# Seven partial products in place of eight for the second products of two token blocks, in five pairs of layer one

## The chip, the cores and the metric

The kernel runs on one core of one Trainium2 chip. The metric is the device time of one execution, in microseconds (us).

## What is computed

Attention with a cluster mask, then two feed-forward layers on 1536 tokens of 512 features (d_ff 2048):

```python
attn_out = _attn_ref(...)                        # 2 x 8 heads x 768 x 64
x = attn_out.transpose(0, 2, 1, 3).reshape(1536, 512)
h = x @ moe_w_in; g = np.maximum(0.01 * h, h); x = g @ moe_w_out          # layer one
h = x @ moe2_w_in; r = np.maximum(h, 0); out = (r * r) @ moe2_w_out       # layer two
```

## The kernel before

Every product in 32-bit precision is made of three matmuls: each operand is split into a high part (rounded to the matmul's format) and a low part (the rest), and high x high, high x low and low x high are summed in PSUM. A matmul has a stationary operand of 128x128 and a moving one of 128x512.

A layer runs over 16 blocks of 128 hidden features, taken in eight pairs, named by their first block, f = 0, 2, ... 14. The tokens are three blocks of 512 (0, 1, 2). In a pair, the first products make h (features x tokens) from the input x; ScalarE writes the activated high part gh and the activated value itself back to PSUM (`acts`, L912), VectorE subtracts them to the low part gl (L934); the second products (`g2`, L945) multiply g by the output weights into four banks o0 to o3 (512 outputs in four slices of 128), summed over the two blocks of the pair, and `flush` (L999) adds each bank into the accumulator `acc` in SBUF on VectorE (L1005).

The pairs f = 0, 2 and 4 of layer one are plain: 3 token blocks x 2 feature blocks x 4 x 3 = 72 matmuls of first products. From f = 6 on `quad` (L1030) makes the first products of token blocks 0 and 1 as a 2 x 2 product of half matrices by Winograd's form of Strassen's rule: seven partial products P1 to P7 of 6 matmuls instead of eight. They go into the banks U, V, W, X (h0 to h3); ScalarE keeps copies of partial sums (L1045, L1056), VectorE adds them (L1038). It needs sums of the input halves (`t_ops`, L1087, worked off over turns by the table `SUMS`, L1192) and sums of the weights, which are a third weight block beside the pair's two (`sum_pieces`, L207). Token block 2 has 24 matmuls. Second products are 72 in every pair, by the plain rule.

A weight block comes by one DMA of 1 MB (SP's queue) as 64-bit words, which are decoded in pieces (`decode_pieces`, L152): load (piece 0), then ScalarE makes the magnitude into wt (L173) and GpSimd the low word (L180) (piece 1), VectorE joins them (L186, piece 2), ScalarE rounds the high part wh (L147, piece 3), GpSimd subtracts the low part wl (L148, piece 4). A sum block has four sums on GpSimd (L221, piece 0), wh (1) and wl (2). The raw words and the words of each of the two blocks have one buffer each; wh and wl go round a ring of RING buffers.

All engines run their instructions in the written order from pair 2 on (`manual_schedule`). `step_list` (L1151) writes a pair as a list of steps, and the loop at the end puts behind step i the pieces of the next pair's weights (`TURN`, L1181) and the sums that SUMS has for that turn; turns are counted over all steps of a layer (pair 0 has ten, pair 2 twelve). The second products of token block 2 of a pair run in the next pair, between its first products.

Of the kernel before, what the change touches and what calls it, by code (L numbers as in the profile page):

```python
# [8 lines left out]
F32 = mybir.dt.float32  # L9
# [54 lines left out]
)  # L64
DOTS = {(0, 0): 0, (0, 1): 1, (1, 0): 2}


@with_exitstack
def attention_moe_moe_kernel(
# [22 lines left out]
    NBLK = NT // N  # L92
    PLAIN = (3, 1)
    EARLY = 1
    RING = 6
    SIDE = 4

    const = ctx.enter_context(tc.tile_pool(name="const", bufs=1))
    const.tile([128, 88], F32, name="cpad")
    xp = ctx.enter_context(tc.tile_pool(name="xp", bufs=1))  # L100
    rpad = ctx.enter_context(tc.tile_pool(name="rpad", bufs=1, side="right"))
    rpad.tile([128, 120], F32, name="rp")
# [104 lines left out]
    def sum_pieces(ci):  # L207

        st = {}
        K = DM // 2  # L210

        def sums():
            w = st["w"] = stg[1].tile([128, 4, K], F32, tag="ws", name="ws")
            t0, t1 = words.pop(ci - 2), words.pop(ci - 1)
            for o, i, k, op in (
                (w[:, 0], t1[:, 0:K], t1[:, K : 2 * K], ALU.add),
                (w[:, 1], w[:, 0], t0[:, 0:K], ALU.subtract),
                (w[:, 2], t0[:, 0:K], t1[:, 0:K], ALU.subtract),
                (w[:, 3], t0[:, K : 2 * K], w[:, 1], ALU.subtract),
            ):  # L220
# [10 lines left out]
        )  # L231


    ast = ctx.enter_context(ExitStack())
    hbp = ast.enter_context(tc.tile_pool(name="hbp", bufs=1))
# [641 lines left out]
    def bank(i):  # L877
        return ps_h.tile([128, N], F32, tag=f"h{i}", name="h")

    def product(out, w, x, first):  # L880
        n = len(w) * 3
        i = 0
        for (ah, al), (bh, bl) in zip(w, x):
            for l, r in ((ah, bh), (ah, bl), (al, bh)):
                nc.tensor.matmul(  # L885
                    out=out, lhsT=l, rhs=r, start=(first and i == 0), stop=(i == n - 1),
                    skip_group_check=not first,
                )
                i += 1
# [49 lines left out]
    def act(m, b, f, h):  # L939
        for g in acts(m, b, f, h):  # L940
            g()
# [85 lines left out]
            r = b * N + o * 128  # L1027
            nc.sync.dma_start(out=out[r : r + 128, part], in_=ob)

    def quad(m, f):  # L1030
        f0, f1, s = ((m, f, j) for j in range(3))
        k2 = range(2)

        def p(out, w, x, first):
            product(out, [w(k) for k in k2], [x(k) for k in k2], first)

        def add(out, a, b):
            nc.vector.tensor_tensor(out=out, in0=a, in1=b, op=ALU.add)  # L1038
# [112 lines left out]
    def step_list(m, f, prev):  # L1151

        def unit(b, j):
            return lambda: act(m, b, f + j, g1(m, b, f + j))

        def out_of(b, j):
            return lambda: g2(m, b, f + j)

        behind = [lambda q=q: g2(*q) for q in prev]
        tail = [(m, 2, f), (m, 2, f + 1)]  # L1160
        if f < 2 * PLAIN[m]:
            seq = [unit(0, 0), unit(0, 1)]
# [7 lines left out]
        first, second, third = quad(m, f)  # L1170
# [132 lines left out]
```

## Time and profile before

| | us |
|---|---|
| median of 3 runs | 752.75 |
| lowest, highest | 749.59, 754.55 |
| the profiled execution | 749.51 |
| its span | 747.7 |

The span runs from the first to the last instruction; 1.8 us of the profiled execution lie around it. Attention takes the first 243 us or so, layer one some 250, layer two 255. Engines: PE = TensorE matmul, PEld = its weight loads, DVE = VectorE, ACT = ScalarE, POOL = GpSimd, SP = the queue that issues DMAs. L963 is line 963 of the code. An engine's busy time is a mean over stages; where one engine is never idle, the others' idle time costs nothing.

### The profile page before, as it was taken

The page shows a single profiled execution, that of the slowest core. Times are in us where ns is not written, and L with a number is a line of the kernel's source. Part 1 is how long each engine was busy: PE and PEld are TensorE (multiplying, and loading weights), DVE is VectorE, ACT ScalarE, POOL GpSimd, SP SyncE. Part 2 cuts the span into 40 slices and gives each one's busy share as a digit, 9 for nine tenths or more (in the row PEclk, how much of TensorE's full clock was granted, in tenths as well). Part 3 has the DMA queues.
Part 4 walks back from the last instruction along what each step waited for, and adds up shares of the span by engine and source line. Part 5 has one row for each costly group of instructions (what it writes and reads, how often), then busy time and mean ns, then how long its engine had stood idle before and what let it go on. Part 6 is the DMA issues. An engine that isn't in the chain of part 4 may idle for free.

```text
span 747.7 us, 11095 instructions
## 1 busy us (share of the span) xinstructions
PE 740.7 (99%) x4044; PEld 646.1 (86%) x4044; DVE 509.6 (68%) x800; ACT 440.7 (59%) x817; POOL 439.6 (59%) x422
## 2 busy tenths in 40 slices
PE   8999999999999999999999999999999999999998
PEld 8999999999998888888888888888888888888886
DVE  7899999999996335666455454563667666576655
ACT  7988988988997553444344343556644335443430
POOL 9999999999866526654342443499434342343400
PEclk9999999999999999999999999999999999999999
DMA  3684574473503311113111131111212112121004
GB/s 109 172 219 114 117 175 117 112 176 77 148 1 114 112 57 57 56 57 113 57 57 57 57 113 56 57 57 57 73 50 103 57 57 66 50 111 56 1 1 169
DMA packets 16406, 64.78 MB, mean 87 GB/s; under 512 B 3040, under 2 KB 4192, under 8 KB 11360
## 3 DMA queue, kind: packets, MB, share of 16 engines
q1 hardware_dynamic: 16352, 64.07, 28.6%
q8 instruction: 32, 0.52, 0.3%
q14 instruction: 22, 0.18, 0.1%
HBM read 43.02 MB, written 3.15 MB: 62 GB/s over the span
## 4 chain that ended last, share of the span: by engine, by line
PE 92%; ACT 3%; DVE 2%; POOL 1%; issue 1%; DMA 0%; POOLq 0%; ACTq 0%; DVEq 0%
PE o L963 34%; PE h L885 33%; PE A L551 8%; PE S L454 7%; PE T L516 7%; PE S L325 1%; ACT e L486 1%; DVE nm L476 1%; PE o L993 1%; DVE el L533 1%; ACT eh L527 0%; POOL e L503 0%; POOL xl L581 0%; POOL hb L650 0%; POOL xh L229 0%
## 5 line engine op out<-in xcount | busy, mean ns | idle before, releaser
L148 POOL TENSOR_TENSOR wl<-wt,wh 128x1024 fp32r<-128x1024 f32 x32 | 76.9, 2402 | 110.4 <-ACT wh L147 110.4
L934 DVE TENSOR_TENSOR gl<-h,gh 128x512 fp32r<-128x512 f32 x96 | 65.6, 690 | 92.8 <-ACT h L929 74.4
L1005 DVE TENSOR_TENSOR acc<-o,acc 128x512 f32<-128x512 f32 x144 | 94.4, 686 | 27.5 <-PE o L963 27.5
L885 PE MATMUL h<-xh,wl 128*128 128x512 f32 x288 | 112.1, 389 | 0.0
L885 PE MATMUL h<-xl,wh 128*128 128x512 f32 x288 | 112.1, 389 | 0.0
L885 PE MATMUL h<-xh,wh 128*128 128x512 f32 x288 | 111.9, 390 | 0.0
L533 DVE TENSOR_TENSOR el<-T,eh 128x512 fp32r<-128x512 f32 x144 | 94.5, 682 | 2.9 <-ACT eh L527 2.3
L503 POOL TENSOR_SCALAR e<-e,r 128x768 f32<-128x768 f32 x96 | 86.2, 908 | 12.6 <-PE T L516 6.8
L476 DVE TENSOR_REDUCE nm<-S 128x1 f32<-128x768 f32 x96 | 90.8, 947 | 3.5 <-PE S L325 1.8
L486 ACT ACTIVATE e<-S,nm 128x768 f32<-128x768 f32 x96 | 87.2, 908 | 9.8 <-DVE ds L353 5.3
L454 PE MATMUL S<-hb 128*128 128x384 f32 x384 | 89.4, 347 | 0.1
L527 ACT CAST eh<-T 128x512 fp32r<-128x512 f32 x144 | 79.6, 590 | 8.7 <-PE T L516 8.6
L928 ACT ACTIVATE gh<-h 128x512 fp32r<-128x512 f32 x48 | 28.7, 597 | 89.6 <-PE h L885 63.8
L551 PE MATMUL A<-eh,vv 128*128 128x256 f32 x288 | 80.3, 308 | 0.6 <-DVE xt L573 0.6
L516 PE MATMUL T<-ident,e 128*128 128x128 f32 x576 | 79.7, 273 | 0.5 <-POOL e L503 0.5
L963 PE MATMUL o<-gl,wh 128*128 128x512 f32 x192 | 74.7, 389 | 0.0
L963 PE MATMUL o<-gh,wl 128*128 128x512 f32 x192 | 74.7, 389 | 0.0
L963 PE MATMUL o<-gh,wh 128*128 128x512 f32 x192 | 73.7, 389 | 0.0
L551 PE MATMUL A<-el,vv 128*128 128x256 f32 x288 | 73.0, 283 | 0.2 <-DVE el L533 0.2
L516 PEld LDWEIGHTS T<-ident,e 128*128 128x128 f32 x576 | 68.9, 143 | 3.6 <-POOL e L503 0.7
L963 PE MATMUL o<-wh,gh 128*128 128x512 f32 x184 | 71.6, 389 | 0.0
L963 PE MATMUL o<-wl,gh 128*128 128x512 f32 x184 | 71.6, 389 | 0.0
(163 smaller groups left out, 1584.5 us busy)
## 6 DMA issues: line engine op xcount, KB each, us to landing
wraw<-w SPq DMA_DIRECT2D x32, 1024.0 KB, 4.7
hb<-spl SPq DMA_DIRECT2D x14, 576.0 KB, 4.7
hb<-spl SPq DMA_DIRECT2D x42, 192.0 KB, 5.1
rqk<-qk SPq DMA_DIRECT2D x16, 384.0 KB, 3.9
rv<-v SPq DMA_DIRECT2D x8, 384.0 KB, 3.3
out<-q SPq DMA_DIRECT2D x11, 256.0 KB, 2.1
hb<-st SPq DMA_DIRECT2D x56, 24.0 KB, 2.2
out<-q SPq DMA_DIRECT2D x2, 128.0 KB, 1.8
```

What stands on the lines that cost most here:

```text
L148: return lambda: nc.gpsimd.tensor_tensor(out=wl, in0=t, in1=wh.bitcast(F32), op=ALU.subtract)
L454: nc.tensor.matmul(out=s[:, c, 0:HALF], lhsT=hb[:, a, i * 128 : (i + 1) * 128], rhs=hb[:, b, c * HALF : (c + 1) * HALF], start=(a == 0), s ...
L476: nc.vector.tensor_reduce(out=n, in_=s_t[t][:, :, 0:HALF], axis=AX.XY, op=ALU.max, negate=True)
L486: nc.scalar.activation(out=e.rearrange("p (a b) -> p a b", a=2), in_=s_t.pop(t)[:, :, 0:HALF], func=AF.Exp, bias=n_t.pop(t), scale=1.0, ac ...
L503: nc.gpsimd.tensor_scalar(out=e_t[t], in0=e_t[t], scalar1=r_t[t // 2][:, t % 2 : t % 2 + 1], scalar2=1.0, op0=ALU.mult, op1=ALU.mult,)
L516: nc.tensor.transpose(T[:, o : o + 128], e_t[2 * u + b][:, kc * 128 : (kc + 1) * 128], ident)
L527: nc.scalar.copy(out=eh[:, 2 * g : 2 * g + 2, :].rearrange("p a b -> p (a b)"), in_=T_t[u, g])
L533: nc.vector.tensor_tensor(out=el[:, 2 * g : 2 * g + 2, :].rearrange("p a b -> p (a b)"), in0=T_t.pop((u, g)), in1=eh[:, 2 * g : 2 * g + 2, ...
L551: nc.tensor.matmul(out=A, lhsT=w, rhs=m[:, kc, :], start=(kc == 0 and i == 0), stop=(kc == KC - 1 and i == 1),)
L885: nc.tensor.matmul(out=out, lhsT=l, rhs=r, start=(first and i == 0), stop=(i == n - 1), skip_group_check=not first,)
L963: nc.tensor.matmul(out=outs[o], lhsT=l, rhs=r, start=(first and i == 0), stop=(last and i == 2),)
L1005: nc.vector.tensor_tensor(out=a, in0=ps, in1=a, op=ALU.add)
```

## The change

In the pairs f = 4, 6, 8, 10, 12 of layer one (`SEVEN`) the second products of token blocks 0 and 1 are seven partial products M1 to M7 by the same rule: B11, B21 (block 0) and B12, B22 (block 1) are the activated values, T1 to T4 their sums, made on VectorE and split like the others; a fourth weight block (index 3) holds the sums of the output weights. M1, M6, M7, M4 add up in one pair of banks (A: o0, o1), M2, then M5 and M3 in the other (B: o2, o3), and after each the running content is added to `acc` (r1.0 is the flush of M1's first half). Block 2's second products are made in the same pair (o0 to o3 of the list, flushed by f0 to f3), no longer in the next. The whole order of such a pair is one list: n, l, c are pieces of the next pair's, the pair after's and this pair's weight blocks, k copies, a adds, h, f and l behind a name its high part, full value and low part. u0 and u1 (token block 2) share bank h1.

```diff
+SEVEN_REST = (
+    "M1 M2 r1.0 r1.1 r2.0 r2.1 B22l l0.0 u1 u1h u1f u1l n2.0 M6 M5 r6.0 r5.0 r5.1 r6.1 n2.1 n2.2 o0 f0 "
+    "M3 r3.0 T4h T4l r3.1 o1 f1 n3.0 M7 r7.0 r7.1 o2 f2 M4 r4.0 r4.1 o3 f3"
+)
+SEVEN_QUAD = (
+    "n0.1 P1 k1 P2 c3.1 c3.2 n0.2 aV n1.0 P6 k6 B11h B11f P5 k5 B11l n0.3 n0.4 P7 aX B22h B22f P3 aW "
+    "B12f P4 B21h B21f T1 T3 B21l T2 n1.1 T1h T2h T1l n1.2 T4 u0 T2l u0h u0f u0l T3h T3l n1.3 n1.4 "
+) + SEVEN_REST
+SEVEN_PLAIN = (
+    "n0.1 g00 B11h B11f c3.1 c3.2 bh0 n0.2 B11l n1.0 g01 B21h B21f B21l bh1 n0.3 n0.4 g10 B12f T1 n1.1 "
+    "n1.2 g11 B22h B22f T3 T2 T1h T2h T1l T4 u0 T2l u0h u0f u0l T3h T3l n1.3 n1.4 "
+) + SEVEN_REST + " h4.0 h4.1"
...
-    RING = 6
+    RING = 7
+    SEVEN = (4, 6, 8, 10, 12)
...
-    const = ctx.enter_context(tc.tile_pool(name="const", bufs=1))
-    const.tile([128, 88], F32, name="cpad")
+    lpad = ctx.enter_context(tc.tile_pool(name="lpad", bufs=1))
+    lpad.tile([128, 96], F32, name="lp")
...
+    ast = ctx.enter_context(ExitStack())
+    hbp = ast.enter_context(tc.tile_pool(name="hbp", bufs=1))
+    const = ast.enter_context(tc.tile_pool(name="const", bufs=1))
+    const.tile([128, 120], F32, name="cpad")
...
+            if m == 0 and f in SEVEN:
+                blocks.append((m, f, 3))
...
-            t0, t1 = words.pop(ci - 2), words.pop(ci - 1)
+            m, f, j = blocks[ci]
+            t0, t1 = (words[blocks.index((m, f, i))] for i in range(2))
+            if j == 2:
+                a11, a12, a21, a22 = t0[:, 0:K], t0[:, K : 2 * K], t1[:, 0:K], t1[:, K : 2 * K]
+            else:
+                a11, a12, a21, a22 = (
+                    t[:, DM + i * K : DM + (i + 1) * K] for i in range(2) for t in (t0, t1)
+                )
...
-    def quad(m, f):
+    def quad(m, f, behind=True):
...
-            act(m, 0, f, V)
+            if behind:
+                act(m, 0, f, V)
...
                 nc.scalar.copy(out=kept[-1], in_=q)
+            if not behind:
+                act(m, 0, f, V)
...
+    def seven(f, prev, after, later):
...
+        ops["aV"] = lambda: add(get("V"), get("V"), st["k1"])
+        ops["aX"] = lambda: add(get("X"), get("U"), st["k5"])
+        ops["aW"] = lambda: add(get("W"), get("W"), st["k6"])
...
+        def active(n, x, sbuf=False):
+            full[n] = tmp("t", 3) if sbuf else x
+            prelu(full[n], x)
+
+        for n, q in (("B11", "V"), ("B21", "U"), ("B22", "X"), ("B12", "W")):
+            ops[n + "h"] = lambda n=n, q=q: high(n, get(q), True)
+            ops[n + "f"] = lambda n=n, q=q: active(n, get(q), n in ("B11", "B12"))
...
+        ops["T1"] = lambda: t_sum("T1", "B12", "B11", "B11")
+        ops["T3"] = lambda: t_sum("T3", "B22", "B12", "B12")
+        ops["T2"] = lambda: t_sum("T2", "B22", "T1", None)
+        ops["T4"] = lambda: t_sum("T4", "B21", "T2", "B21")
...
+        for n in ("B11", "B21", "B22", "T1", "T2", "T3", "T4", "u0", "u1"):
+            eng = nc.gpsimd if n in ("B11", "T1", "T2", "T3") else nc.vector
+            ops[n + "l"] = lambda n=n, eng=eng: low(n, eng)
...
+        for name, q, block, c, g, b, half in (
+            ("1", "A", f0, DM, "B11", 0, 0), ("2", "B", f1, DM, "B21", 0, 0),
+            ("6", "A", so, K, "T2", 1, 0), ("5", "B", so, 0, "T1", 1, 1),
+            ("3", "B", so, 3 * K, "B22", 1, 0), ("7", "A", so, 2 * K, "T3", 1, 1),
+            ("4", "A", f1, DM + K, "T4", 0, 1),
+        ):
...
-            11: "w12.0 w11.0", 12: "t1.0 w22.0", 13: "t2.0 h1.0", 14: "l1.0 h2.0",
-            15: "t3.0 w21.0", 16: "l2.0 h3.0", 17: "t4.0", 18: "l3.0",
-            22: "w12.1 w11.1", 23: "t1.1 w22.1", 24: "t2.1 h1.1", 25: "l1.1 h2.1",
-            26: "t3.1 w21.1", 27: "l2.1 h3.1", 28: "t4.1", 29: "l3.1", 30: "h4.0", 31: "h4.1",
+            7: "w12.0 w11.0", 8: "t1.0 w22.0", 9: "t2.0 h1.0", 10: "l1.0 h2.0",
+            11: "t3.0 w21.0", 12: "l2.0 h3.0", 13: "t4.0", 14: "l3.0",
+            15: "w12.1 w11.1", 16: "t1.1 w22.1", 17: "t2.1 h1.1", 18: "l1.1 h2.1",
+            19: "t3.1 w21.1", 20: "l2.1 h3.1", 21: "t4.1 l3.1",
...
-            seq, prev = step_list(m, f, prev)
...
+            if m == 0 and f in SEVEN:
+                seven(f, prev, after, later)
+                prev = []
+                continue
+            seq, prev = step_list(m, f, prev)
...
+                if m == 0 and i == 8 and f + 2 == SEVEN[0]:
+                    piece((*after, 3), 0)
```

## Rows read from the trace of the kernel before

**Rows 1.** The page's table of busy time: us, share of the span, instructions.
```profile
PE 740.7 (99%) x4044; PEld 646.1 (86%) x4044; DVE 509.6 (68%) x800; ACT 440.7 (59%) x817; POOL 439.6 (59%) x422
```

**Rows 2.** Busy time by stretch, one pair: busy us (instructions), granted clock, DMA share.
```profile
341.56:372.84 31.28, 31.28 (x140) 25.90 (x139) 16.45 (x24) 13.15 (x20) 12.28 (x10) 1.00 0.20 69
```

**Rows 3.** The chain in order of time, layer one: start, us, what.
```profile
341.56 4.08 PE h L885 x18
...
372.84 4.08 PE h L885 x18
```

**Rows 4.** Timeline, layer one: start us, us, engine, line, operation [idle before].
```profile
333.01 0.39 PE L885 MATMUL h<-xh,wl 128*128 128x512 f32 x1
...
333.50 0.70 DVE L1038 TENSOR_TENSOR h<-h,q 128x512 f32<-128x512 f32 x1 [1.10 <-ACT q L1045]
...
343.89 0.39 PE L885 MATMUL h<-xh,wl 128*128 128x512 f32 x1
344.12 0.39 PE L885 MATMUL h<-xh,wh 128*128 128x512 f32 x1
...
344.32 0.70 DVE L1038 TENSOR_TENSOR h<-h,q 128x512 f32<-128x512 f32 x1 [0.60 <-PE h L885]
...
344.93 0.68 DVE L934 TENSOR_TENSOR gl<-h,gh 128x512 fp32r<-128x512 f32 x1
...
345.05 0.60 ACT L928 ACTIVATE gh<-h 128x512 fp32r<-128x512 f32 x1 [0.22 <-DVE h L1038]
...
345.55 0.59 ACT L929 ACTIVATE h<-h 128x512 f32<-128x512 f32 x1
```

**Rows 5.** Groups of instructions: xcount, busy us, mean ns, idle before; one DMA line.
```profile
L885 PE MATMUL h<-xh,wh 128*128 128x512 f32 x288 | 111.9, 390 | 0.0
...
L1005 DVE TENSOR_TENSOR acc<-o,acc 128x512 f32<-128x512 f32 x144 | 94.4, 686 | 27.5 <-PE o L963 27.5
...
L148 POOL TENSOR_TENSOR wl<-wt,wh 128x1024 fp32r<-128x1024 f32 x32 | 76.9, 2402 | 110.4 <-ACT wh L147 110.4
...
L147 ACT CAST wh<-wt 128x1024 fp32r<-128x1024 f32 x32 | 33.7, 1053 | 1.7 <-DVE wt L186 1.7
...
L221 POOL TENSOR_TENSOR ws<-wt 128x256 f32<-128x256 f32 x24 | 17.6, 735 | 57.9 <-DVE wt L186 57.9
...
wraw<-w SPq DMA_DIRECT2D x32, 1024.0 KB, 4.7
```

**Rows 6.** Timeline: a weight block's high part on ACT, GpSimd behind it.
```profile
339.36 1.05 ACT L147 CAST wh<-wt 128x1024 fp32r<-128x1024 f32 x1
...
340.50 2.40 POOL L148 TENSOR_TENSOR wl<-wt,wh 128x1024 fp32r<-128x1024 f32 x1 [11.64 <-ACT wh L147]
342.98 1.10 POOL L180 TENSOR_SCALAR wraw<-wraw 128x1024 int32<-128x1024 uint32 x1
```

**Rows 7.** Timeline, pairs 4 and 6: VectorE with two SBUF operands beside GpSimd.
```profile
303.79 1.22 DVE L186 SCALAR_TENSOR_TENSOR wt<-wt,wraw 128x1024 int32<-128x1024 int32 x1
304.92 1.78 DVE L1097 TENSOR_TENSOR q<-xh,xl 128x512 f32<-128x512 f32 x1
...
313.41 1.46 DVE L1097 TENSOR_TENSOR q<-xh,xl 128x512 f32<-128x512 f32 x1
314.79 2.30 DVE L186 SCALAR_TENSOR_TENSOR wt<-wt,wraw 128x1024 int32<-128x1024 int32 x1
...
303.96 2.20 POOL L1103 TENSOR_TENSOR q<-q 128x512 f32<-128x512 f32 x1 [10.55 <-DVE q L1097]
...
313.02 1.30 POOL L1103 TENSOR_TENSOR q<-q 128x512 f32<-128x512 f32 x1
314.28 1.74 POOL L1109 TENSOR_TENSOR tl<-q,th 128x512 fp32r<-128x512 f32 x1
```

**Rows 8.** Timeline: GpSimd's longest wait in layer one; two sums' low parts on VectorE.
```profile
272.89 1.29 POOL L1103 TENSOR_TENSOR q<-q 128x512 f32<-128x512 f32 x1 [14.32 <-DVE q L1097]
...
325.15 4.25 DVE L1147 TENSOR_TENSOR xl<-t,xh 128x512 fp32r<-128x512 f32 x2 [0.78 <-ACT xh L1146]
```

More of the change, by code (lines that the diff above doesn't have):

```diff
@@ L213, in sums @@
             w = st["w"] = stg[1].tile([128, 4, K], F32, tag="ws", name="ws")
-            t0, t1 = words.pop(ci - 2), words.pop(ci - 1)
+            m, f, j = blocks[ci]
[6 more added lines that the diff above has]
+                )
             for o, i, k, op in (
[L216 to L219, printed above, removed]
+                (w[:, 0], a21, a22, ALU.add),
+                (w[:, 1], w[:, 0], a11, ALU.subtract),
+                (w[:, 2], a11, a21, ALU.subtract),
+                (w[:, 3], a12, w[:, 1], ALU.subtract),
             ):
@@ L231, in pool_copy @@
         )
-    ast = ctx.enter_context(ExitStack())
-    hbp = ast.enter_context(tc.tile_pool(name="hbp", bufs=1))
     vp = ast.enter_context(tc.tile_pool(name="vp", bufs=2))
@@ L1085, in quad, with add, get, prod @@
         return first, second, third
+    def seven(f, prev, after, later):
+        f0, f1, si, so = ((0, f, j) for j in range(4))
+        k2, ks = range(2), range(HP)
+        K = DM // 2
+        st = {}
+        ops = {}
+        def add(out, a, b, op=ALU.add):
+            nc.vector.tensor_tensor(out=out, in0=a, in1=b, op=op)
+        def get(n):
+            if n not in st:
+                st[n] = bank("UVWX".index(n))
+            return st[n]
+        def prod(n, w, x, first):
+            product(get(n), w, x, first)
+        def keep(n, key):
+            st[key] = tmp()
+            nc.scalar.copy(out=st[key], in_=get(n))
+        first_products = {
+            "P1": ("U", lambda k: w_in(f0, k), lambda k: x_in(k, 0), True),
+            "P2": ("V", lambda k: w_in(f0, 2 + k), lambda k: x_in(2 + k, 0), True),
+            "P6": ("U", lambda k: w_in(si, 2 + k), lambda k: t_in(1, k), False),
+            "P5": ("W", lambda k: w_in(si, k), lambda k: t_in(0, k), True),
+            "P7": ("U", lambda k: w_in(si, 4 + k), lambda k: t_in(2, k), False),
+            "P3": ("W", lambda k: w_in(si, 6 + k), lambda k: x_in(2 + k, 1), False),
+            "P4": ("U", lambda k: w_in(f1, 2 + k), lambda k: t_in(3, k), False),
+        }
+        for name, (n, w, x, fresh) in first_products.items():
+            ops[name] = lambda n=n, w=w, x=x, fresh=fresh: prod(
+                n, [w(k) for k in k2], [x(k) for k in k2], fresh
+            )
+        for name, n, b, block in (
+            ("g00", "V", 0, f0), ("g01", "U", 0, f1), ("g10", "W", 1, f0), ("g11", "X", 1, f1)
+        ):
+            ops[name] = lambda n=n, b=b, block=block: prod(
+                n, [w_in(block, k) for k in ks], [x_in(k, b) for k in ks], True
+            )
+        for name, n in (("k1", "U"), ("k6", "U"), ("k5", "W")):
+            ops[name] = lambda name=name, n=n: keep(n, name)
+        ops["aV"] = lambda: add(get("V"), get("V"), st["k1"])
+        ops["aX"] = lambda: add(get("X"), get("U"), st["k5"])
+        ops["aW"] = lambda: add(get("W"), get("W"), st["k6"])
+        def prelu(out, x):
+            nc.scalar.activation(out=out, in_=x, func=AF.Prelu, alpha=0.01)
+        hi, lo, full = {}, {}, {}
+        def high(n, x, active=False):
+            hi[n] = gg.tile([128, N], F32R, tag="gh", name="gh")
+            lo[n] = gg.tile([128, N], F32R, tag="gl", name="gl")
+            if active:
+                prelu(hi[n], x)
+            else:
+                nc.scalar.copy(out=hi[n], in_=x)
+        def low(n, eng):
+            eng.tensor_tensor(out=lo[n], in0=full[n], in1=hi[n].bitcast(F32), op=ALU.subtract)
+        def active(n, x, sbuf=False):
[4 more added lines that the diff above has]
+            ops[n + "f"] = lambda n=n, q=q: active(n, get(q), n in ("B11", "B12"))
+        def t_sum(out, x, y, to):
+            full[out] = tmp("t", 3) if to is None else full[to]
+            add(full[out], full[x], full[y], ALU.subtract)
+        ops["T1"] = lambda: t_sum("T1", "B12", "B11", "B11")
+        ops["T3"] = lambda: t_sum("T3", "B22", "B12", "B12")
+        ops["T2"] = lambda: t_sum("T2", "B22", "T1", None)
+        ops["T4"] = lambda: t_sum("T4", "B21", "T2", "B21")
+        for n in ("T1", "T2", "T3", "T4"):
+            ops[n + "h"] = lambda n=n: high(n, full[n])
+        def unit(j):
+            st[f"u{j}"] = bank(1)
+            product(
+                st[f"u{j}"], [w_in((f0, f1)[j], k) for k in ks], [x_in(k, 2) for k in ks], True
+            )
+        for j in range(2):
+            n = f"u{j}"
+            ops[n] = lambda j=j: unit(j)
+            ops[n + "h"] = lambda n=n: high(n, st[n], True)
+            ops[n + "f"] = lambda n=n: active(n, st[n])
+        for n in ("B11", "B21", "B22", "T1", "T2", "T3", "T4", "u0", "u1"):
+            eng = nc.gpsimd if n in ("B11", "T1", "T2", "T3") else nc.vector
+            ops[n + "l"] = lambda n=n, eng=eng: low(n, eng)
+        def second(out, ws, g, fresh, stop=True):
+            wh, wl = ws
+            mm = ((wh, hi[g]), (wh, lo[g]), (wl, hi[g]))
+            for i, (l, r) in enumerate(mm):
+                nc.tensor.matmul(
+                    out=out, lhsT=l, rhs=r, start=(fresh and i == 0), stop=(stop and i == 2),
+                    skip_group_check=True,
+                )
+        def w_out(block, c):
+            return tuple(w[:, c : c + 128] for w in weights[block])
+        def seventh(q, block, c, g, fresh):
+            if fresh:
+                for j in range(2):
+                    i = 2 * "AB".index(q) + j
+                    st[q, j] = (ps_l if i == 3 else ps_o).tile(
+                        [128, N], F32, tag=f"o{i}", name="o"
+                    )
+            for j in range(2):
+                second(st[q, j], w_out(block, c + 128 * j), g, fresh)
+        for name, q, block, c, g, b, half in (
[3 more added lines that the diff above has]
+            ("4", "A", f1, DM + K, "T4", 0, 1),
+        ):
+            ops["M" + name] = lambda q=q, block=block, c=c, g=g, name=name: seventh(
+                q, block, c, g, name in "125"
+            )
+            for j in range(2):
+                ops[f"r{name}.{j}"] = lambda q=q, j=j, b=b, o=2 * half + j: flush(
+                    0, b, f // 2, o, st[q, j]
+                )
+        def last(o):
+            ps = st["o", o] = bank((3, 2, 3, 2)[o])
+            c = DM + o * 128
+            second(ps, w_out(f0, c), "u0", True, False)
+            second(ps, w_out(f1, c), "u1", False)
+        for o in range(4):
+            ops[f"o{o}"] = lambda o=o: last(o)
+            ops[f"f{o}"] = lambda o=o: flush(0, 2, f // 2, o, st["o", o])
+        for i, q in enumerate(prev):
+            ops[f"bh{i}"] = lambda q=q: g2(*q)
+        for c, base in (("n", after), ("l", later), ("c", (0, f))):
+            for k in range(4):
+                for j in range(5):
+                    ops[f"{c}{k}.{j}"] = lambda base=base, k=k, j=j: piece((*base, k), j)
+        for kk in range(2):
+            ops[f"h4.{kk}"] = t_by[0][kk]["h4"]
+        for name in (SEVEN_PLAIN if f < 2 * PLAIN[0] else SEVEN_QUAD).split():
+            ops[name]()
@@ L1168, in step_list @@
             return seq, tail
-        first, second, third = quad(m, f)
+        first, second, third = quad(m, f, bool(behind))
+        behind = behind or [lambda: None] * 2
         seq = [
@@ L1211, in piece @@
             i = blocks.index(block)
-            pieces[block] = (sum_pieces if block[2] == 2 else decode_pieces)(i)
+            pieces[block] = (sum_pieces if block[2] > 1 else decode_pieces)(i)
         pieces[block][j]()
```

## Prediction

> **What bounds the kernel now.** I read the busy table first: TensorE (PE) is busy 99% of the 747.7 us span, the others 59 to 68% [rows 1]. Then the table by stretches: in one pair of layer one (f = 6 to 12 are four alike) PE is busy 31.28 of 31.28 us, VectorE 16.45, ScalarE (ACT) 13.15, GpSimd 12.28, and the granted clock is 1.00, the 2.4 GHz level [rows 2]. Then the chain in order of time: nothing but matmuls, back to back. From one pair's 18-matmul run (341.56) to the next pair's (372.84) are 31.28 us [rows 3]; a pair has 66 first and 72 second products, 138 matmuls, so one costs 31.28 / 138 = 0.2267 us. Its row says 390 ns [rows 5], but that is its length in the pipe; neighbours start 0.23 us apart [rows 4]. So in layer one a matmul removed is worth 0.2267 us, as long as the other engines have the next operand ready.
>
> **What the change removes.** A pair's second products of blocks 0 and 1 are 2 features x 2 blocks x 4 outputs x 3 = 48 matmuls. Seven products of 2 halves x 3 make 42. Six fewer in each of five pairs: 30 x 0.2267 = **6.80 us**. First products (72 in pair 4, 66 later) and block 2's 24 stay. The pair is then 132 matmuls, 29.92 us.
>
> The Trainium skill (TensorE: Matmul & The Clock Gate, "Wait — 56ns, not 53.3ns?") gives warm matmuls of 512 columns 215.7 ns from start to start; by that the 30 would give 6.47 us. The rows of this case differ from it, and they decide.
>
> **What it adds, beside PE.** By durations of [rows 5], for a pair of seven:
> - VectorE: 18 flushes into acc instead of 12, four sums T1 to T4, five low parts, three adds of products (aV, aX, aW), 30 x about 0.69 = 20.7, and two joins of a weight block's words at 1.22 [rows 7]: 23.1 of 29.92 us (78%).
> - GpSimd: the fourth weight block's sums (4 x 0.74) and low part (2.40), four low parts of 512 columns at 1.30 [rows 7], on top of 12.28: 22.8 of 29.92 (76%).
> - ScalarE: one more weight copy (1.05), four T copies, one prelu less (0.60 each [rows 4]): +2.9 on 13.15, 16 of 29.92.
> No engine is full, so these cost nothing unless the order makes PE wait. I count a pair f = 6 to 12 from its first matmul, by its written order. PE's places are multiples of 6 matmuls (1.36): P1 0, P2 1.36, P6 2.72, P5 4.08, P7 5.44, P3 6.80, P4 8.16, u0 9.52, M1 12.24, M2 13.60, u1 14.96, M6 17.68. Links from [rows 4]: a reader of a product starts 0.43 after its last matmul's start (343.89 to 344.32; once 0.49, 333.01 to 333.50), ACT 0.03 after DVE, neighbours on ACT 0.50 and on DVE 0.61 apart; GpSimd follows ACT by 0.09 (339.36 + 1.05 to 340.50) and itself by 0.08 where the operation changes [rows 6].
>
> **The tight place is u1.** It writes the bank that u0 used, so it needs u0's low part (u0l, VectorE) done; behind u1 in PE's queue stands the rest of the pair, M6 to o3. Backwards: T1 needs B12's prelu. P3's last matmul starts at 7.93; aW at 8.36 to 9.06; B12f to 9.69; T1 asks at 9.72. From there VectorE is a row: T1, T3, B21l (B21f ends 10.82), T2, the join of the next block, T4, u0l.
>
> T1 and the join read two SBUF tensors, and the trace shows what that means beside GpSimd [rows 7]: a join that begins with GpSimd idle takes 1.22 and the GpSimd operation begun 0.17 later takes 2.20 instead of 1.30; a sum asked for at 304.92 ends at 306.70, 0.54 behind that operation's end at 306.16; the join at 314.79 takes 2.30, ending 1.07 behind GpSimd's end at 316.02. They take turns, and a waiting VectorE operation goes ahead of GpSimd's next (the sum at 313.41 ends at 314.87, 0.55 behind one GpSimd operation's end, and the next, at 314.28, takes 1.74). Operations with a PSUM operand show none of it (0.69). The Trainium skill (GPSIMD Engine Reference, "Key points") says that GpSimd shares its SBUF interfaces with VectorE, in contention with instructions that have two SBUF inputs; the trace agrees, and this rule speaks against the change.
>
> So who is first? GpSimd's chain starts from P6: k6 at 4.28, B11h 4.78, B11f 5.28, k5 5.78, weight copy 6.28 to 7.33, the weight's low part 7.42 to 9.82, its next operation (the raw words' low half, 1.10 [rows 6]) at 9.90. T1 asks at 9.72, so it runs 9.82 to 10.37, ahead of that 1.10. Then T3 10.35, B21l 10.97, T2 11.59, the join 12.20 (GpSimd idle: its T1l waits for T1h, 11.8 to 12.4 on ACT behind B21f and n1.1) to 13.42, T4 13.35, u0l 13.97 to 14.66. u1 is due at 14.96. The trace has no row for PE's release by VectorE; between 0 and 0.3 it costs nothing. Stall: **0**, but by margins of 0.1 to 0.3 us.
>
> **Other places.** Flushes between M1 and M4: behind u0l VectorE has r1, r2 and B22l (5 x 0.61, to 17.7), u1l when ACT has u1f (19.0) to 19.7, then r6.0, r5.0 to 21.0; M3, which adds into that bank, is due at 21.8. r7.0 follows at 25.9 to 26.6; M4, which adds into its bank, is due at 27.2. No stall, 0.6 to 0.8 us spare; if late, their price is the lateness. GpSimd, from the join's end at 13.4: T1l, T2l, T3l to 17.3, a low part to 19.6, four sums to 22.4, a copy on ACT to 23.5, the low part to 26.0, the fourth block's sums to 28.8. Those read the words that ACT's first instruction of the next pair (n0.1, 1.1 us) rewrites, and behind it stands k1, due at 31.5: 1.6 us spare. Loads: SP's next load waits for the join at 13.4, lands 4.7 us later [rows 5], needed at 29.9. Pair 4 (plain first products) has 24 more matmuls of pair 2's tails between the links: u1 due 0.4 us behind u0l. Pair 14 lost the second products that stood between its first ones; each of its copies (0.60) lies under a product (1.36): k6 at 4.28 to 4.87, P7 at 5.44. The sums for the quads move from turns 11 to 31 into 7 to 21: GpSimd idles 14.32 and 10.55 us there [rows 7, 8]; nothing to at most one pair of two-SBUF operations (4.25 [rows 8]), taken at nothing. The last of them (h4) stands ahead of pair 6's join: the same 4.25 if GpSimd is in the way, 1.1 if not, and P3 waits only from about 2.4 on: 0 to 1.8, taken 0. Moved constants, longer ring: layout only, 0.
>
> **Sum.** 749.51 (span 747.7 and 1.8 around it) - 6.80 = 742.7 for the profiled execution. That lies 3.2 us under the median of the runs, 752.75, and at their lowest, 749.59. On the median: 752.75 - 6.80 = **746.0**, 0.9% less. A measurement of this kernel tells about 1% from no change.
>
> **Rivals.**
> 1. *T1 loses its turn*: it asks 0.1 us too late, waits for the 1.10 us operation, T1 ends near 11.5, u0l near 15.9, u1 waits 1.2 to 1.4. Four pairs: 5.2. Net -1.6: 751.2. For it: the margin is below what one link varies (0.43 or 0.49 after a matmul). Against: the varying link moves GpSimd's chain too, and a T1 that waits wins.
> 2. *Both turns lost, slower than before*: the join too then stands behind T1l (1.31): u1 waits about 2.5 in four pairs, 10.0 against 6.80: +3.2, 756.0. It decides from 1.7 us a pair (6.80 / 4). Against: the join asks only when T2 is done, 0.2 us before T1l.
> 3. *GpSimd's queue is the bound*: 23 us of 29.92 and the turns it gives up (about 2) leave few us; its sums end over 2 us late, n0.1 on ACT holds k1, P6 waits, 1 us a pair in four, and pair 6's h4 takes 1.8: -6.8 + 5.8: 751.8. For: the share. Against: the spare 1.6 us.
> 4. *The 30 matmuls don't give their time*, because their intervals become waits for flushes: 752.75. VectorE's share of 78% speaks for it, the spare 0.6 us against.
>
> **How the numbers follow.** Forecast 0.60; rival 1 0.20; rival 2 0.06; rival 3 0.07; rival 4 0.07. The likeliest spans 742.8 (lowest run less 6.80) to 748; rivals 1, 3 and 4 end by 753. Range 742 to 753, leaving out rival 2 and some of each end. Faster by over 1% (under 745.2) wants 7.5 us, more than the sum, and comes only from the runs' spread: 0.25. Slower by over 1% (760.3) wants 14.3 us of stalls, beyond rival 2: 0.05. Within 1%: 0.70.
>
> **What would show it.** Right: from one quad pair's P1 to the next 29.9 us; PE busy 29.9 of it; T1 about 0.6 long with its GpSimd neighbour at 1.6 instead of 1.1; u0l ending 0.3 us before u1. Rival 1: T1 near 1.7 and a gap before u1's first matmul of 1.2 us, released by VectorE's u0l. Rival 2: the join near 2.4 as well. Rival 3: gaps before P6 and n0.1 waiting for GpSimd's sums. Rival 4: gaps before M3, M4 or M7. Wrong altogether: a matmul interval other than 0.2267, or a time below 740.

## The result, and the profile after

| | median, us | lowest to highest | runs |
|---|---|---|---|
| before | 749.85 | 749.54 to 754.55 | 6 |
| after | 744.13 | 743.81 to 747.96 | 6 |

The ratio is 0.991, with an interval of 0.9881 to 0.9939, all of it below 1. By the medians it is 5.7 us less (0.8%), somewhat under the 1% that the prediction gave as what a measurement of this kernel tells from no change. The forecast was 746.0, on a median of 752.75; 749.85 - 6.80 would have been 743.05. In size the forecast was 6.80 us less and 5.7 came.

The busy table of the changed kernel's page, where [rows 1] had PE 740.7, VectorE 509.6, ACT 440.7, GpSimd 439.6:

```profile
PE 738.1 (99%) x4014; PEld 643.1 (86%) x4014; DVE 534.6 (72%) x845; ACT 453.2 (61%) x837; POOL 497.6 (67%) x467
```

PE has 30 instructions less, as counted; VectorE and GpSimd have 25 and 58 us more and are still far from full. PE's busy time fell by 2.6 us only. The table by stretches says why (columns: us, then busy us and instructions of PE, PEld, DVE, ACT, POOL, then granted clock, DMA share, GB/s):

```profile
9.00:15.00 6.00, 6.00 (x29) 5.72 (x29) 3.72 (x11) 2.54 (x4) 5.54 (x4) 0.50 0.00 0
...
302.91:339.63 36.72, 36.72 (x163) 30.42 (x163) 23.05 (x35) 15.52 (x24) 26.11 (x21) 1.00 0.17 58
339.63:369.60 29.97, 29.97 (x133) 24.70 (x133) 22.44 (x34) 15.74 (x24) 23.93 (x18) 1.00 0.21 71
459.51:491.36 31.85, 31.57 (x139) 25.83 (x139) 17.45 (x24) 19.02 (x30) 16.41 (x11) 1.00 0.25 87
```

The first line is an accident of this one execution: PE's clock was at 0.50 (the 1.2 GHz level) from 9 to 15 us, in attention, and the execution took 747.96 us. The same kernel profiled again lacks it: a span of 742.2, a clock of 1.00, and PE busy for 735.4 us, 5.3 less than before. Executions of both kernels are now and then 2 to 7 us longer, by attention where a trace shows it, so I read stages, take sums from the span of 742.2, and read differences of tenths between the fastest executions.

The line 339.63:369.60 is the answer to [rows 2]: the same pair, 29.97 us instead of 31.28, PE busy for all of it, VectorE 22.44 (predicted 23.1), ACT 15.74 (16), GpSimd 23.93 (22.8). Pair 4 (302.91 to 339.63) has 162 matmuls, 162 x 0.2267 = 36.73: nothing is lost in it, h4 at its end included.

The chain of waits in order of time (start, us, what). [rows 3] had runs of 18 matmuls 31.28 apart; a quad pair now opens with 54 first products in a row:

```profile
247.61 2.76 PE h L910 x12
...
254.49 1.30 POOL q L1285
255.79 0.60 POOL xh L256
...
257.00 2.26 POOL q L1285
259.25 1.81 POOL xl L606
...
261.09 1.56 ACT acc L1027 x3
...
263.66 0.51 ACT gh L953
...
264.21 1.20 PE o L988 x4
...
339.63 12.24 PE h L910 x54
...
354.59 2.77 PE h L910 x12
...
369.60 12.24 PE h L910 x54
```

The two runs of 54 begin 29.97 us apart: that is the gain. The lines before them, in pair 0, are a loss that I had not seen: the chain leaves PE and runs through two GpSimd sums of the input halves (L1285). In GpSimd's queue one stands ahead of the first operation of attention's last split (L256 xh), the other between it and the second (L606 xl). ACT's copies into acc wait for that split, and behind them, with a sum's high part in their row (L1288), ACT's gh is late for PE. Here the split's second operation begins at 259.21 and the copies at 261.09, in an execution that is 4.1 us late by then. The kernel before (its timeline):

```profile
251.59 2.73 POOL L581 TENSOR_TENSOR xl<-xt,xh 128x768 fp32r<-128x768 f32 x1
...
253.61 1.56 ACT L1002 COPY acc<-o 128x512 f32<-128x512 f32 x3
```

There the copies begin 0.71 before the split ends (254.32): they don't wait for it. In the changed kernel they begin 0.03 behind its end, and so they do in other kernels below with its layout (split's end and first copy at 257.01 and 257.04 without pairs of seven, at 255.01 and 255.04 with the two sums moved). So the wait itself came with the new layout. By the order of the pools in the code the longer ring moves acc by one buffer towards the last of attention's tiles; that this, and not another of the moves, brings the wait, no run shows.

The tight place of the prediction, in the timeline of the first quad pair (here P1's first matmul starts at 339.46):

```profile
346.82 2.39 POOL L168 TENSOR_TENSOR wl<-wt,wh 128x1024 fp32r<-128x1024 f32 x1
349.26 0.69 DVE L1124 TENSOR_TENSOR t<-t 128x512 f32<-128x512 f32 x1 [0.73 <-POOL wl L168]
349.29 1.66 POOL L200 TENSOR_SCALAR wraw<-wraw 128x1024 int32<-128x1024 uint32 x1
...
351.79 1.22 DVE L206 SCALAR_TENSOR_TENSOR wt<-wt,wraw 128x1024 int32<-128x1024 int32 x1
...
353.60 0.69 DVE L1177 TENSOR_TENSOR gl<-h,gh 128x512 fp32r<-128x512 f32 x1
354.42 0.42 PE L910 MATMUL h<-xh,wh 128*128 128x512 f32 x1
354.68 0.39 PE L910 MATMUL h<-xl,wh 128*128 128x512 f32 x1
```

T1 (L1124) begins 9.80 after P1 (predicted 9.82) and wins its turn: it takes 0.69, and GpSimd's next operation, begun 0.03 later, takes 1.66 where it takes 1.10 alone [rows 6]. The join (351.79) takes 1.22, as predicted. u0's low part (L1177) ends at 354.29, 14.83 after P1 (predicted 14.66). u1's first matmul starts at 14.96, on time, but only 0.13 behind it, and the second follows 0.26 later instead of 0.23: in the chain these twelve take 2.77 instead of 2.72, 0.05 a pair (2.80, 0.08 a pair, in the second profile).

Pair 14, where the prediction had a cost of nothing:

```profile
465.95 0.61 ACT L954 ACTIVATE h<-h 128x512 f32<-128x512 f32 x1
...
466.59 0.69 DVE L959 TENSOR_TENSOR gl<-h,gh 128x512 fp32r<-128x512 f32 x1 [2.44 <-ACT h L954]
467.20 1.29 DVE L1063 TENSOR_TENSOR h<-h,q 128x512 f32<-128x512 f32 x2
...
467.94 0.50 PE L910 MATMUL h<-xh,wh 128*128 128x512 f32 x1 [0.28 <-DVE h L1063]
```

PE's last partial product waits for a VectorE sum (L1063) that stands behind a low part (L959), which itself waits for two activations on ACT (L953, L954). The change had put these two behind the copies wherever no second products stand between the first (`if not behind`). Its place in the pair is known: P1 at 459.51, 138 matmuls, due to end at 459.51 + 31.28 = 490.79; it ends at 491.36, so 0.57 us are lost.

The sum, at the last VectorE operation of the kernel, where nothing but a store is to come. In the chain of before, and of the changed kernel profiled again with PE's clock at 1.00 throughout:

```profile
744.23 0.42 DVE q L1026
```

```profile
739.12 0.42 DVE q L1051
```

That is 5.11 less. The account, in this second execution: 6.80 - 0.8 (pair 0) - 0.6 (pair 14) - 0.3 (u1, 0.08 in each of four pairs) = 5.1. Pair 0's 0.8: first products end at 255.88 in the chain, 42 matmuls more (9.52) are due to end at 265.40, and the next run begins at 266.19. The spans differ by 747.7 - 742.2 = 5.5: what comes behind the last operation, 747.7 - 744.23 = 3.47 before, is 3.08 after. So 0.4 of the gain is in the last store, which the change doesn't touch; why, I can't say.

### The profile page after: what moved, and what is told of

Same layout as the page of the kernel before. It is cut to its first block, busy times and chain, and to the rows that moved or that the text cites. A ratio compares the mean times of both kernels' runs of the same rounds, so it can differ in the third digit from the quotient of the medians.

```text
span 746.2 us, 11181 instructions
## 1 busy us (share of the span) xinstructions
PE 738.1 (99%) x4014; PEld 643.1 (86%) x4014; DVE 534.6 (72%) x845; ACT 453.2 (61%) x837; POOL 497.6 (67%) x467
## 4 chain that ended last, share of the span: by engine, by line
PE 91%; ACT 3%; DVE 3%; POOL 2%; issue 1%; DMA 0%; POOLq 0%; DVEq 0%; ACTq 0%
PE h L910 32%; PE o L988 23%; PE A L576 8%; PE S L479 7%; PE T L541 7%; PE o L1217 6%; PE h L1217 4%; PE S L350 1%; ACT e L511 1%; DVE nm L501 1%; PE o L1018 1%; DVE el L558 1%; PE dots L350 1%; POOL xl L606 0%; POOL q L1285 0%
## 5 line engine op out<-in xcount | busy, mean ns | idle before, releaser
L1030 DVE TENSOR_TENSOR acc<-o,acc 128x512 f32<-128x512 f32 x154 | 100.0, 685 | 11.8 <-PE o L988 11.8
L528 POOL TENSOR_SCALAR e<-e,r 128x768 f32<-128x768 f32 x96 | 86.4, 911 | 12.7 <-PE T L541 6.8
L959 DVE TENSOR_TENSOR gl<-h,gh 128x512 fp32r<-128x512 f32 x66 | 45.0, 691 | 54.0 <-ACT h L954 35.6
L988 PE MATMUL o<-wh,gl 128*128 128x512 f32 x184 | 71.6, 389 | 0.0
L944 ACT ACTIVATE t<-h 128x512 f32<-128x512 f32 x48 | 28.0, 599 | 71.3 <-PE h L910 38.0
L168 POOL TENSOR_TENSOR wl<-ws,wh 128x1024 fp32r<-128x1024 f32 x17 | 41.4, 2433 | 38.2 <-ACT wh L167 38.2
L910 PEld LDWEIGHTS h<-xh,wh 128*128 128x128 f32 x288 | 54.1, 188 | 12.4 <-DVE gl L1177 0.7
```

What stands on the lines that cost most here:

```text
L168: return lambda: nc.gpsimd.tensor_tensor(out=wl, in0=t, in1=wh.bitcast(F32), op=ALU.subtract)
L528: nc.gpsimd.tensor_scalar(out=e_t[t], in0=e_t[t], scalar1=r_t[t // 2][:, t % 2 : t % 2 + 1], scalar2=1.0, op0=ALU.mult, op1=ALU.mult,)
L910: nc.tensor.matmul(out=out, lhsT=l, rhs=r, start=(first and i == 0), stop=(i == n - 1), skip_group_check=not first,)
L988: nc.tensor.matmul(out=outs[o], lhsT=l, rhs=r, start=(first and i == 0), stop=(last and i == 2),)
L1030: nc.vector.tensor_tensor(out=a, in0=ps, in1=a, op=ALU.add)
```

## The experiments

All kernels below are the changed one with the edit shown. The changed one itself ran again (x0): median 744.36, the fastest six 743.97 to 744.32, ratio to before 0.9938, interval 0.9918 to 0.9958. It ran on the chip of the two runs with late sums and of the one with pair 14's order alone; the others ran on two more chips. Before's fastest on the three are 749.46, 749.48 and 749.42, so a tenth between chips means nothing.

> The change as it is, for comparison. By the account of its first trace: 30 matmuls less give 6.80 us, of which pair 0 loses 0.75 (ScalarE's copies into acc wait for GpSimd's last split of attention), pair 14 loses 0.57 (a product waits for VectorE) and the four waits before u1 lose 0.05 each: 5.3 us less than before. If the shortfall were only the spread of runs, 6.8 less.

### Without any pair of seven, and with two

```diff
-    SEVEN = (4, 6, 8, 10, 12)
+    SEVEN = ()
...
-            19: "t3.1 w21.1", 20: "l2.1 h3.1", 21: "t4.1 l3.1",
+            19: "t3.1 w21.1", 20: "l2.1 h3.1", 21: "t4.1 l3.1", 30: "h4.0", 31: "h4.1",
...
-                if m == 0 and i == 8 and f + 2 == SEVEN[0]:
+                if m == 0 and i == 8 and SEVEN and f + 2 == SEVEN[0]:
```

> No pair with seven products; the other edits stay (ring of 7, constants in attention's space, sums at turns 7 to 21, words kept). Theory: the sums in pair 0 cost their 0.75 us here too, the layout nothing: 750.2 to 750.6 in its fastest group where the kernel before has 749.5. Rival (layout or ring give or take something of their own): outside 749.9 to 750.9.

Measured: median 749.97, fastest 749.90; ratio to before 1.0003 (0.9982 to 1.0024). Before's fastest beside it is 749.48: 0.4 slower, less than I expected. The chain tells why:

```profile
266.25 2.72 PE h L910 x12
...
745.08 0.42 DVE q L1051
```

In before the run at 266.25 begins at 265.40, and the last operation at 744.23: 0.85 later in both places. So pair 0's wait is there in full and nothing else is lost or gained up to the last operation; behind it are 748.2 - 745.08 = 3.12, as short as in the change. Layout and moved sums gain nothing by themselves; together they cost pair 0's 0.85, and the 6.80 less the stalls sits in the pairs of seven.

With two pairs (`SEVEN = (4, 6)`):

> Only pairs 4 and 6 have the seven partial products. Mine: each such pair gives its six matmuls in full, 12 x 0.2267 = 2.72 us, and the stall that the changed kernel has in pair 14 (0.57) comes now in pair 8, the first pair behind a seven-pair, whose first products then stand next to one another; the bank of u1 costs 0.05 in one pair. From the fastest runs without any such pair (749.90): 749.90 - 2.72 + 0.57 + 0.05 = 747.8. Rival 1: what the five pairs gave together is shared evenly: (749.9 - 744.0) x 2 / 5 = 2.4, 747.5 and no wait in pair 8. Rival 2: the stall belongs to the seam before layer two and not to the pair behind a seven-pair: 747.2, and a wait in pair 14 at most.

Measured: median 747.97, five of ten runs at 747.76 to 747.88; ratio 0.9984 (0.9959 to 1.0009). 747.8 is met, and the wait is where it was expected, in pair 8 (timeline of this kernel):

```profile
377.92 0.69 DVE L959 TENSOR_TENSOR gl<-h,gh 128x512 fp32r<-128x512 f32 x1 [2.44 <-ACT h L954]
...
378.53 1.29 DVE L1063 TENSOR_TENSOR h<-h,q 128x512 f32<-128x512 f32 x2
...
379.27 0.50 PE L910 MATMUL h<-xh,wh 128*128 128x512 f32 x1 [0.28 <-DVE h L1063]
```

The same 2.44 and 0.28 as in pair 14. So six matmuls a pair come off in full, and the loss of 0.57 belongs to the pair that follows a pair of seven, whichever it is: PE's list of waits has this one once, and none in pair 14.

### Pair 14: the sum ahead of the low part

```diff
-                act(m, 0, f, V)
+                kept.append(acts(m, 0, f, V))
+                kept[-1].pop(0)()
...
-            u2, p5 = kept
+            u2, p5, *v = kept
...
             add(X, U, p5)
+            for q in v:
+                q.pop(0)()
```

> In pair 14 the low part of B11 on VectorE stands behind the sum aX instead of ahead of it. Theory: PE's gap of 0.57 us before P4 goes, 0.5 to 0.6 us under the change. Rival (P4 would wait for another engine next, or the gap is the record's): same as the change within 0.2.

Measured: the fastest three of six 743.34 to 743.52, 0.6 under the change's 743.97; median 744.42, ratio 0.9933 (0.9907 to 0.9959). PE's wait for L1063 is gone from its list of waits. The interval alone doesn't show 0.6; the fastest runs and the list do.

### Pair 0: the sums later

First all sums of the first half squeezed into later turns:

```diff
-            7: "w12.0 w11.0", 8: "t1.0 w22.0", 9: "t2.0 h1.0", 10: "l1.0 h2.0",
...
+            10: "w12.0 w11.0", 11: "t1.0 w22.0", 12: "t2.0 h1.0", 13: "l1.0 h2.0 t3.0 w21.0",
+            14: "l2.0 h3.0 t4.0", 15: "l3.0 w12.1 w11.1", 16: "t1.1 w22.1", 17: "t2.1 h1.1",
...
```

> The input sums for the quads moved from turns 7 to 21 into turns 10 to 21, so that none stands in pair 0. Theory: pair 0's 0.75 us comes back, 0.7 to 0.8 us under the change, and the trace has PE without a gap from the last matmul of attention on, as before. Rival (the wait in pair 0 comes from the memory layout, or the shortfall is spread): same as the change within 0.2.

Measured: fastest 746.99, median 749.73, ratio 0.999 (0.9966 to 1.0013): 3.0 slower than the change. A miss. Pair 0's wait went, but another came (timeline, pair 2 of this kernel):

```profile
300.95 0.62 ACT L1288 CAST th<-q 128x512 fp32r<-128x512 f32 x1 [4.75 <-POOL q L1285]
...
302.58 0.69 DVE L959 TENSOR_TENSOR gl<-h,gh 128x512 fp32r<-128x512 f32 x1 [8.19 <-ACT h L954]
...
303.33 0.50 PE L910 MATMUL h<-xh,wh 128*128 128x512 f32 x1 [3.33 <-DVE gl L959]
...
303.92 0.63 PE L910 MATMUL h<-xh,wl 128*128 128x512 f32 x1
304.34 0.63 PE L910 MATMUL h<-xh,wh 128*128 128x512 f32 x1
```

Squeezed, GpSimd's sums run late; ACT stands 4.75 us at a sum's high part that waits for one (L1288 behind L1285), and the activation of the pair's own last block is queued behind it on ACT. 3.3 less the 0.75 gained would be 746.5; 747.0 came. The median is higher for another reason: behind the wait the granted clock is 0.50, the 1.2 GHz level, from 304 to 307, matmuls start 0.42 us apart instead of 0.23 (303.92, 304.34), and these twelve take 4.61 us in the chain instead of 2.72. Of the twelve executions only the two fastest (746.99, 747.17) have a mean clock of 1.00; the next three are 748.47 to 748.60, at 0.997 to 0.998. So the sums had a cost on both sides: too early they hold attention's split, too late they hold pair 2.

The same with pair 14's order and u1's bank (below):

> Late sums, pair 14's order, and u1 in bank h2 instead of u0's h1, together. Theory: all of 0.75 + 0.57 + 4 x 0.05 = 1.5 us comes back, PE without a gap through layer one, 1.4 to 1.6 us under the change and 6.8 to 7.2 under the kernel before. Rival (the gains overlap or another wait comes next): less than 1 us under the change.

Measured: fastest 746.19, median 747.69, ratio 0.9973 (0.9946 to 0.9999); the wait is there again, 3.4 us, and the clock's fall behind it. Its fastest is 0.8 under that of the run above, about what the two other edits give by themselves below and above (0.4 and 0.6).

Then only the two sums that had stood beside the split, with the high part that stood behind them (`h1.0`):

```diff
-            7: "w12.0 w11.0", 8: "t1.0 w22.0", 9: "t2.0 h1.0", 10: "l1.0 h2.0",
+            7: "w12.0 w11.0", 8: "w22.0", 10: "t1.0 t2.0 h1.0 l1.0 h2.0",
```

> Only the first two GpSimd sums of the input halves move, from turns 8 and 9 to turn 10. Mine: pair 0's waits before its second block of second products go (0.75 us) and nothing comes in their place: fastest runs near 743.2 against 744.0 of the change, the rest of the trace as in the change. Rival: what was gained by moving all three things together came from pair 14 and the bank alone, and GpSimd's later sums make another wait in pair 2, as squeezing them did: 744.0 or more, with a wait in pair 2.

Measured: median 743.30, fastest 743.19, 0.78 under the change's 743.97; ratio 0.991 (0.9887 to 0.9934). PE's wait for gh in pair 0 is gone. In its timeline the split and the copies come early again, and the sums behind them:

```profile
252.30 2.71 POOL L606 TENSOR_TENSOR xl<-xt,xh 128x768 fp32r<-128x768 f32 x1
...
255.04 1.57 ACT L1027 COPY acc<-o 128x512 f32<-128x512 f32 x3 [0.67 <-POOL xl L606]
...
259.25 2.67 POOL L1285 TENSOR_TENSOR q<-q 128x512 f32<-128x512 f32 x2
```

The copies still wait for the split, but it is early enough to cost PE nothing. The high part (L1288), which took 0.52 us of the row on ACT in pair 0, moved along with the sums; what each of the two gives alone, the run doesn't tell.

### The tight place: T1 made to lose its turn

One GpSimd operation (c3.2, the fourth block's low part) goes two steps later, so that GpSimd is busy when T1 asks; then the same with a bank of its own for u1:

```diff
-    "n0.1 P1 k1 P2 c3.1 c3.2 n0.2 aV n1.0 P6 k6 B11h B11f P5 k5 B11l n0.3 n0.4 P7 aX ...
+    "n0.1 P1 k1 P2 c3.1 n0.2 aV n1.0 P6 k6 B11h B11f P5 k5 B11l n0.3 c3.2 n0.4 P7 aX ...
...
-            st[f"u{j}"] = bank(1)
+            st[f"u{j}"] = bank(1 + j)
```

> Only GpSimd's order changes: the low part of the fourth weight block (2.40 us) stands behind B11l instead of ahead of it, in the four pairs 6 to 12. It then ends about 0.1 us before T1 asks, and the next low part (2.40) has begun. Theory (turns at the shared interface, a begun GpSimd operation is not broken off): T1 waits for it, starts 2.0 to 2.2 us later than in the change, u0l and u1 follow, PE stands 2.0 to 2.3 us before u1 in each of four pairs, 8 to 9 us slower than the change: 752 to 753. Rival (T1 shares the interface, or its turn was not what kept u1 on time): T1 at most 0.7 longer, under 3 us in all.

> As the run before, and u1 in bank h2, which is free from B12's prelu on, instead of u0's h1. Theory (u1 waited only for u0's bank): no wait before u1; T1 as late as there; VectorE's row then reaches the flushes of M1 and M2 late, and M6 and M5 wait for them, about 0.9 us a pair, 3.6 in all: 4 to 5 us faster than the run before. Rival (u1 waits for something else too, or the lost turn costs elsewhere in full): as slow as the run before within 1 us.

Measured, first the order alone: median 759.50, fastest 758.0, ratio 1.0101 (1.0065 to 1.0137): not 8 but 14 to 15 us slower than the change. The timeline of its first quad pair (335.54 to 369.43 in the chain), and two matmuls of the second:

```profile
344.93 2.40 POOL L168 TENSOR_TENSOR wl<-wt,wh 128x1024 fp32r<-128x1024 f32 x1
345.18 2.71 DVE L1124 TENSOR_TENSOR t<-t 128x512 f32<-128x512 f32 x1 [0.73 <-ACT t L1164]
...
351.85 0.68 DVE L1177 TENSOR_TENSOR gl<-h,gh 128x512 fp32r<-128x512 f32 x1
...
352.58 0.77 PE L910 MATMUL h<-xh,wh 128*128 128x512 f32 x1 [1.87 <-DVE gl L1177]
...
386.80 0.63 PE L910 MATMUL h<-xl,wh 128*128 128x512 f32 x1
387.23 0.63 PE L910 MATMUL h<-xh,wl 128*128 128x512 f32 x1
```

and the first pair's stretches:

```profile
335.54:352.00 16.46, 15.17 (x67) 11.97 (x65) 11.82 (x14) 11.08 (x19) 10.17 (x6) 1.00 0.20 64
352.00:353.00 1.00, 0.42 (x1) 0.42 (x2) 1.00 (x2) 0.97 (x2) 1.00 (x2) 0.82 0.71 139
353.00:356.00 3.00, 3.00 (x8) 2.35 (x8) 2.51 (x5) 0.00 (x0) 3.00 (x3) 0.50 0.75 306
356.00:369.43 13.43, 13.43 (x60) 11.09 (x60) 9.57 (x15) 3.78 (x5) 9.25 (x11) 1.00 0.01 2
```

T1, asked for 0.25 after GpSimd's operation began, takes 2.71 and ends 0.56 behind that operation's end (347.33): rival 1's mechanism, made on purpose. Counted from P1, T1 ends 2.0 later than in the change and u0's low part 2.3 later, and u1 is held by it, PE idle for 1.87, as expected. What was not expected is the third line: behind that wait the granted clock is 0.50, the 1.2 GHz level, and neighbouring matmuls start 0.43 apart instead of 0.23 (386.80, 387.23), eight or nine of them in each of the four pairs. The first pair is 33.89 us, 4.0 more than the 29.92 without stalls. From u1's first matmul (352.58) to the next pair's first (369.27 in the timeline) are 16.69 for 66 matmuls, 66 x 0.2267 = 14.96, so 1.7 are the clock's. The last matmul before u1 starts at 350.31, so u1 was due at 350.54, and 2.0 are the wait's; the other 0.2 are lost ahead of it, in M2, behind B21's late low part. Two of the five executions are 1.4 us faster, at a mean clock of 0.993 instead of 0.991, as if one fall of the four were missing in them (an estimate).

With the second bank: median 746.84 (746.72 to 747.07), ratio 0.9947 (0.9926 to 0.9967). T1 is as late (2.71 again), there is no wait before u1, the clock stays at 1.00, and 12.7 us come back, not the 4 to 5 expected. What is left against the change, 2.8, is 0.7 a pair (30.7 us from one to the next in the chain): in the chain's second quad pair M1 and M2 take 0.19 more than their matmuls, M6 and M5 0.15, and 0.40 is lost ahead of M4 and in it, whose wait (0.15 in the first quad pair) ends with a flush into acc. So it was the shared bank that turned T1's lateness into the wait before u1, and with it into the clock's fall.

The bank alone, with the order of the change:

> Only u1's bank changes (h2 in place of h1). Mine: the pair of seven goes from 29.97 to 29.92 us, 4 x 0.05 = 0.2 less in the whole, fastest runs 743.8; pair 0 and pair 14 as in the change. Rival: u0's flush was not what u1 waited for, and the pair stays at 29.97, or bank h2 is needed sooner for something else and the pair gets longer.

Measured: median 743.72, fastest 743.61, 0.4 under the change; ratio 0.9926 (0.99 to 0.9953). The quad pair begins at 335.58 and the next at 365.50: 29.92, as forecast without any stall.

### The three small losses taken out together

The bank, pair 14's order and the two sums, in one kernel:

> The first two GpSimd sums moved out of pair 0 to pair 2's first turn, where GpSimd idles 8.6 us, the rest of the sums as in the change; pair 14's B11l behind aX; u1 in bank h2. Theory: 0.75 + 0.57 + 4 x 0.05 = 1.5 us under the change, fastest group of runs at 742.3 to 742.6 where the change has 743.8 to 744.3; PE without a gap through layer one. Rival (GpSimd in pair 2 has no room for 2.6 us more): a wait of PE in pair 2 or 4, no faster than the change.

Measured: median 742.49, fastest 742.35; ratio 0.9907 (0.9876 to 0.9937). It beats both kernels, the changed one by 1.6 us, about the sum of its parts alone (0.4 + 0.6 + 0.8). Its waits of PE in layer one are none, and its quad pairs in the chain:

```profile
339.89 12.24 PE h L910 x54
369.81 12.24 PE h L910 x54
399.73 12.24 PE h L910 x54
429.65 12.24 PE h L910 x54
```

29.92 apart, all four. From before's 749.48 to 742.35 are 7.13 us: with the stalls gone, the 30 matmuls give the 6.80 forecast, and the last store the 0.3 more (3.14 us behind the last operation).

## Why the prediction was right, and where not

**The matmuls.** Right: 0.2267 us each, in full. The period without stalls is 29.92 in two kernels; in the change it is 29.97 to 30.00, by u1. Two pairs of seven gave 2.72 less the stall behind them. Rival 4 (intervals that turn into waits) is out: pair 4 is 36.72 for 36.73 of matmuls.

**T1's turn and u1.** Right in mechanism, and in time to 0.02 us for T1 and 0.17 for u0l. The forecast of no stall was off by a little: with u0l 0.17 late, the release of PE by VectorE, which I had bounded by 0 and 0.3 and put inside the margin, no longer fits into it. That costs 0.05 to 0.08 a pair (0.3 to 0.4 in the whole, by the run with the other bank). The Trainium skill (SBUF - State Buffer, "SBUF: two separate sides") calls the port pair that VectorE and GpSimd share an exclusive lock, held for a whole instruction, the other one fully blocked. The runs agree: T1 ended 0.56 behind the 2.40 us operation that it had met 0.25 after its start.

**Rival 1's price** leaves out the clock. The forecast took a lost turn at 1.3 us a pair, the wait alone; a turn lost to an operation of 2.40 costs 2.0 by the wait before u1, 0.2 ahead of it and 1.7 by the clock behind it. No step of the prediction counted the clock, because in [rows 2] PE never stops. For the 1.10 us operation of the rival itself no run was made, so whether a wait of 1.3 would lower the clock too is open. Rival 2 (both turns lost) has a wait of 2.5, between two behind which the clock fell (1.87 and 3.33); by that it would have been dearer than its 10 us, which is an estimate.

**Pair 14** was the step that failed: "each of its copies (0.60) lies under a product (1.36)" looked at ACT alone. It left out VectorE's queue: with the second products gone from between, the low part of block 0, waiting for two activations that now stand behind ACT's copies, stands in front of the sum that PE needs. 0.57 us, shown by reordering the low part and the sum (0.6), and by ending the pairs of seven with pair 6 (the stall moved to pair 8). A pair 14 with the activations left ahead of the copies was not run.

**The moved sums** were "taken at nothing", with a bound of 4.25. The idle time of GpSimd in [rows 8] was real, but the place that mattered was earlier: in turns 8 and 9 attention's last split is still to come in the same queue, and the copies into acc now wait for it. 0.8, shown by moving the two sums alone, and by the run without pairs of seven, which has it too. "Layout only, 0" is the other half of this miss: in the kernel before the copies don't wait for the split, so the new layout brought the wait and the moved sums made it long. With the sums moved out of its way the layout costs PE nothing; the moved sums with the old layout were not run.

**Flushes, GpSimd's queue, h4:** no stall in the quads, and none at pair 4's end, as forecast; rival 3 is out, though GpSimd's load was 1.1 us more than counted. (VectorE's 23.1 of 29.92 is 77%, not 78%; nothing hangs on it.)

**The size.** 6.80 forecast, 5.5 to 5.7 measured: three stalls take 1.7 from it, and a shorter last store gives 0.4. The absolute time was forecast on 752.75, a median of three runs of which two were above 752; six runs put it at 749.85. So the base was 2.9 too high and the gain 1.1 too large, and 744.13 lay 1.9 under the forecast: that it came this near is in part luck, since the two errors go opposite ways.

## What to carry to other kernels

When work is taken out from between an engine's instructions, go through each other engine's queue once more: what used to be finished under it now stands in front of what is needed next (pair 14). Work moved into idle time of an in-order queue has to be checked against what comes behind it there, back to the first thing that a later stage waits for (pair 0), and against what it feeds, if moved the other way (pair 2). A new layout can make one engine wait for another where none did before (pair 0 again). Where a margin is a tenth of a microsecond, give the reader its own buffer: the bank made the same late operation cost 0.7 us a pair instead of 3.9.

## What the runs showed of the hardware

TensorE's granted clock fell to 0.50 behind a wait of 1.87 us in an otherwise full stretch, and eight or nine matmuls started 0.43 us apart before it was back at 1.00, in four pairs out of four of the profiled execution; the lost clock (1.7 us) cost nearly as much as the wait (2.0). Behind the 3.33 us of the late sums it fell to 0.50 too, but two of that kernel's twelve executions have a mean clock of 1.00. With waits of 0.15 to 0.28 us (pair 14, the late flushes) it stayed at 1.00, and so it did behind one of 1.60 us in attention (in the run of pair 14's order). The Trainium skill (TensorE: Matmul & The Clock Gate, "Why this matters for your kernels") warns of idle gaps of the PE in the middle of a kernel. The 1.87 us here is shorter than the gaps that it names, and the runs decide.

VectorE's turn against GpSimd depends on who began: 0.03 us ahead of GpSimd's operation the same T1 takes 0.69, 0.25 us behind it 2.71.
